# Grouped-query attention on one core: V loaded 8 KB per partition, scores in 32x64 tiles, PV by row halves, Q turned by a 0/1 matmul

## The chip, the core and the metric

The kernel runs on one core of a Trainium2 chip. The core has a matrix engine (TensorE, "PE" in the profile; its weight loads are listed apart as "PEld"), a vector engine (DVE), an activation engine (ACT), GpSimd (POOL) and a sync engine (SP) that issues all DMAs here. Sixteen DMA engines carry the data between HBM and the on-chip buffer SBUF. TensorE writes its results to PSUM, from where DVE or ACT have to fetch them. The metric is the device time of one execution in microseconds (us), as the median of several runs; lower is better.

## What is computed

```python
B, Hq, Hkv, Sq, Sk, D = 16, 32, 8, 16, 2048, 128      # q, k, v in bfloat16
def reference(q, k, v):
    rep = Hq // Hkv                                   # 4 query heads for one K/V head
    k = jnp.repeat(k, rep, axis=1)
    v = jnp.repeat(v, rep, axis=1)
    scores = jnp.einsum("bhqd,bhkd->bhqk", q, k) * D ** -0.5
    p = softmax(scores, axis=-1)
    return jnp.einsum("bhqk,bhkd->bhqd", p, v)
```

There are 128 K/V heads (16 x 8). Each has 64 query rows (4 query heads x 16 positions), 2048 keys of 128 numbers, and as many values. K and V are 67 MB each and every byte is used once, so the data has to stream through.

## The kernel before, in words

**Units.** A *quad* is four K/V heads, and there are NQD = 32 of them; a *pair p* is two heads, and there are NP = 64. K comes a quad at a time (2 MB, 16 KB in each of 128 partitions, a head in 32 partitions), V a pair at a time (1 MB). For V the 2048 keys of a head are spread over all 128 partitions, 16 keys in each, so a partition gets 4 KB for each of the two heads. Q comes in chunks of 16 heads (8 pairs).

**Stages of the work.**
- *KT* (line 351, DVE): 32x32 transposes turn half of a quad's keys into KT, as fp32 words that hold two bf16 numbers each. The head stays in its 32 partitions, and the 128 dimensions lie as 32 partitions x 2 (b) x 2 (e). Two instructions for each score step.
- *Q* (line 174; DVE for chunk 0, POOL for the rest): `lay_q` lays Q out with zeros at the other heads' places (Q4), through a mask. TensorE turns it (line 278: four stages of four fp32 transposes for a chunk) and ACT copies it out of PSUM into QT (line 404).
- *S(n)* (lines 300 and 256, TensorE): scores of half of a quad's keys for its four heads. A matmul has 64 contraction rows (two heads, with a block-diagonal Q of 128 columns) and 512 keys; two row tiles (64x128) run side by side. 16 matmuls; every second group uses weights that are already loaded (line 256).
- *Sneg* (line 373, DVE): two instructions fetch S(n) from PSUM, scale it by minus the softmax scale and keep the minimum; every second n a small instruction (line 381) makes the softmax shift of the quad.
- *exp(p)* (line 413, ACT): 2048 exponentials for each row, with the row sum.
- *PT* (line 312, TensorE): eight fp32 transposes turn the exponentials of a pair in two halves of four; ACT copies each half out of PSUM (line 423). The two halves and the Q stages share NSTAGE = 3 PSUM banks in turn (`free(u)` waits until the use three earlier has been copied out).
- *PV(p)*: 16 keys of each partition. In the wide form (line 330) one matmul has both heads' weights (128 columns) and both heads' values (256 columns), and half of its result is not used. In the narrow form (line 336) there are two column tiles of 64, one for each head. `both_heads` (line 29) takes the wide form in three pairs out of four until the last eight pairs.
- *norm(p)* (lines 436 and 440, ACT; the last five on DVE, line 394): result times the reciprocal of the row sum (line 359), then a 32 KB store.

**Order.** Each engine runs its list in order, and semaphores tie the lists. `pe_prog` and `act_prog` are written by one loop (lines 136 to 145): for p it emits S(p+2), exp(p), PV(p-4), norm(p-4), the two halves PT(p), and in the steps p = 2, 3, 4, 5 of eight one of the four Q stages. The first score step of a chunk, S(8c), waits for the last Q copy (line 287). DVE runs Sneg of n and then KT of n+2. PV(p) waits until norm(p-1) has emptied the one PSUM bank of results (line 322).

**DMA.** SP issues everything in one list (lines 238 to 247). K has NK = 3 buffers and waits for the KT of three quads earlier, V has NV = 7 buffers of one pair and waits for the PV of seven pairs earlier, stores wait for their norm. The last pair's V comes in two parts (LASTV).

## Time and profile before

| | |
|---|---|
| median of 3 runs | 342.75 us (342.29 to 343.37) |
| span of the profiled execution | 340.7 us, so some 2 us lie around it |
| PE busy | 304.3 us (89%) |
| DVE busy | 304.8 us (89%) |
| ACT busy | 253.6 us (74%) |
| DMA | 138.87 MB, mean 408 GB/s; 16 engines 99.5% covered by packets |
| granted TensorE clock | 0.5 between 12 and 24 us, 1.00 from 27 us on |

The main loop repeats every eight pairs, with the chunk of Q: the first score step of a chunk starts at 54.19, 94.02, 133.83, 173.65, 213.47, 253.29 and 293.11 us, so a period is 39.82 us and one pair 4.98 us. "Busy" for PE covers the way of a matmul through the array, so starts of successive groups say more than durations. In a row of the timeline the first number is the start, the second the time until the last of its instructions has ended, and the bracket holds the idle time of the engine just before and what ended it.

### The profile page before, as it was taken

The numbers are of one execution on the slowest core, as the hardware profiler recorded it, in microseconds if no ns is written. First come the engines' busy times: TensorE is split into PE (matmuls) and PEld (weight loads), VectorE is DVE, ScalarE is ACT, GpSimd is POOL, SyncE is SP. The second block draws the span as 40 slices with busy tenths as digits, with TensorE's granted clock in tenths as the row PEclk, the third lists the DMA queues.
The fourth block names the chain that finished last, engine by engine and source line by source line (L and its number), as shares of the span: only waits on it lengthen the run. The fifth ranks groups of instructions, "written<-read, shape, count | busy, mean of one in ns | idle before, by whom it ended". The sixth has DMA issues, their size and how long they took to land.

```text
span 340.7 us, 7084 instructions
## 1 busy us (share of the span) xinstructions
PE 304.3 (89%) x3040; PEld 182.4 (54%) x2528; DVE 304.8 (89%) x457; ACT 253.6 (74%) x390; POOL 81.3 (24%) x40
## 2 busy tenths in 40 slices
PE   3466798999899998999989999999989999899987
PEld 3012355555655664566555556556645665555556
DVE  1879998999989997999989999899979999899952
ACT  3025776789777888778867897778887788678875
POOL 2840007500092004900075000920039000000000
PEclk9759999999999999999999999999999999999999
DMA  7999999999999999999999999999999999999993
GB/s 294 443 415 420 425 415 414 411 419 422 424 423 410 415 419 424 416 420 407 419 426 423 419 405 417 421 428 415 412 418 416 426 418 423 408 419 415 410 407 121
DMA packets 32688, 138.87 MB, mean 408 GB/s; under 512 B 10896, under 2 KB 11152, under 8 KB 28560
## 3 DMA queue, kind: packets, MB, share of 16 engines
q1 hardware_dynamic: 32656, 138.42, 99.5%
q8 instruction: 22, 0.36, 0.4%
q14 instruction: 10, 0.08, 0.1%
HBM read 136.31 MB, written 2.10 MB: 406 GB/s over the span
## 4 chain that ended last, share of the span: by engine, by line
PE 55%; DVE 28%; ACT 9%; issue 5%; DMA 2%; ACTq 0%; SPq 0%; DVEq 0%
PE O_ps L330 17%; DVE Sneg L373 17%; PE S_ps L300 14%; PE S_ps L256 12%; DVE KT L351 11%; PE ST_ps L312 8%; ACT P L413 4%; ACT QT L404 2%; DMA Kn<-in_k_dram 2%; PE ST_ps L278 2%; ACT PT L423 2%; ACT O L436 1%; PE S_ps L336 1%; PE O_ps L336 1%; DVE rrec L359 0%
## 5 line engine op out<-in xcount | busy, mean ns | idle before, releaser
L373 DVE TENSOR_SCALAR_CACHE_REDUCE Sneg<-S_ps 128x1024 f32<-128x1024 f32 x128 | 150.7, 1213 | 19.1 <-PE S_ps L256 18.9
L351 DVE STREAM_TRANSPOSE KT<-Kn 128x1024 f32<-128x1024 f32 x128 | 150.8, 1217 | 3.9 <-DMA Kn<-in_k_dram 3.9
L413 ACT ACTIVATE P<-Sneg,nbias 128x2048 bf16<-128x2048 f32 x64 | 128.2, 2004 | 16.1 <-DVE nbias L381 15.1
L300 PE MATMUL S_ps<-KT,QT 64*128 64x512 bf16 x512 | 103.5, 394 | 24.1 <-DVE Sneg L373 12.8
L174 POOL TENSOR_SCALAR Q<-Qn,mask 128x1024 bf16<-128x1024 bf16 x28 | 79.1, 2843 | 181.1 <-PE ST_ps L278 174.6
L256 PE MATMUL S_ps<-KT,QT 64*128 64x512 bf16 x512 | 103.1, 392 | 0.0
L330 PEld LDWEIGHTS O_ps<-Vb,PT 128*128 128x128 bf16 x672 | 62.4, 98 | 34.7 <-issue 28.0
L330 PE MATMUL O_ps<-Vb,PT 128*128 128x256 bf16 x672 | 80.7, 273 | 0.0
L423 ACT ACTIVATE PT<-ST_ps 128x512 f32<-128x512 f32 x128 | 69.3, 595 | 13.1 <-PE ST_ps L312 12.1
L300 PEld LDWEIGHTS S_ps<-KT,QT 64*128 64x128 bf16 x512 | 27.4, 94 | 93.7 <-issue 72.4
L312 PE MATMUL ST_ps<-ident,P 128*128 128x128 f32 x512 | 67.6, 275 | 4.1 <-ACT P L413 4.1
L436 ACT ACTIVATE O<-O_ps,rrec 64x128 bf16<-64x128 f32 x84 | 30.4, 362 | 46.2 <-PE O_ps L330 45.7
L312 PEld LDWEIGHTS ST_ps<-ident,P 128*128 128x128 f32 x512 | 56.9, 141 | 10.3 <-ACT P L413 7.8
L278 PE MATMUL ST_ps<-ident,Q 128*128 128x128 f32 x128 | 20.4, 291 | 5.2 <-DVE Q L174 5.2
L404 ACT ACTIVATE QT<-ST_ps 128x512 f32<-128x512 f32 x32 | 19.3, 604 | 5.1 <-PE ST_ps L278 5.1
L336 PEld LDWEIGHTS O_ps<-Vb,PT 128*64 128x64 bf16 x576 | 16.7, 110 | 11.5 <-issue 11.5
L336 PE MATMUL O_ps<-Vb,PT 128*64 128x128 bf16 x576 | 19.5, 221 | 0.6 <-ACT O L440 0.6
L278 PEld LDWEIGHTS ST_ps<-ident,Q 128*128 128x128 f32 x128 | 16.4, 152 | 5.2 <-issue 5.2
L413 ACT ACTIVATION_READ_ACCUMULATOR P<-Sneg,nbias 128x1 f32 x64 | 12.2, 191 | 0.0
L373 DVE DVE_READ_ACCUMULATOR Sneg<-S_ps 128x1 f32 x128 | 10.6, 83 | 0.0
L440 ACT ACTIVATE O<-O_ps,rrec 128x128 bf16<-128x128 f32 x17 | 6.0, 351 | 2.2 <-PE O_ps L336 2.2
L381 DVE TENSOR_TENSOR nbias<-nhalf 128x2 f32<-128x2 f32 x32 | 5.1, 160 | 1.1
(19 smaller groups left out, 20.1 us busy)
## 6 DMA issues: line engine op xcount, KB each, us to landing
Kn<-in_k_dram SPq DMA_DIRECT2D x32, 2048.0 KB, 15.3
Vb<-in_v_dram SPq DMA_DIRECT2D x63, 1024.0 KB, 16.6
Qn<-in_q_dram SPq DMA_DIRECT2D x8, 256.0 KB, 13.3
out_dram<-O SPq DMA_DIRECT2D x64, 32.0 KB, 16.1
Vb<-in_v_dram SPq DMA_DIRECT2D x1, 768.0 KB, 12.0
Vb<-in_v_dram SPq DMA_DIRECT2D x1, 256.0 KB, 12.3
```

The source lines that it names most:

```text
L174: eng.tensor_scalar(Q4[:, :, :, r, :].rearrange("p j b x -> p (j b) x"), src, mask[:, r:r + 1], None, op0=ALU.mult,).then_inc(sem_q4, 1)
L256: return pe.add_instruction(mybir.InstMatmult(name=nc.get_next_instruction_name(), engine=mybir.EngineType.PE, ins=[pe.lower_ap(rhs), pe.l ...
L278: ins = pe.transpose(dst[:, 128 * j:128 * (j + 1)], src[:, 4 * x + j, b, :], ident4[:, :])
L300: ins = pe.matmul(s_ap, w, x, start=(acc == 0), stop=(acc == 3))
L312: ins = pe.transpose(dst[:, 128 * t:128 * (t + 1)], P[p % 2][:, 128 * x:128 * (x + 1)], ident4[:, :])
L330: ins = pe.matmul(O_ps[:, 0:256], pt[:, j // 2, j % 2, :], Vb[p % NV][:, :, j, :], start=(j == 0), stop=(j == J - 1),)
L336: ins = pe.matmul(o_ap(p)[64 * g:64 * (g + 1), :], pt[:, j // 2, j % 2, 64 * g:64 * (g + 1)], Vb[p % NV][:, g, j, :], start=(j == 0), stop ...
L351: dve.transpose(KT[n % NKT][:, :].rearrange("p (t b g e a) -> p e g t b a", t=J // 4, b=2, g=4, e=2)[:, e], Kn[Q % NK][:, :].bitcast(F32). ...
L373: dve.tensor_scalar(Sneg[p % NS][:, 1024 * x:1024 * (x + 1)].rearrange("p (t a m) -> p t a m", t=4, m=8), S_ps[:, 1024 * y:1024 * (y + 1)] ...
L413: act.activation(P[p % 2][:, :].bitcast(BF16), Sneg[p % NS][:, :], ACT.Exp, bias=nbias[:, p:p + 1], scale=-1.0, accum_out=rowsum[:, p:p + ...
L423: act.activation(PT[p % NPT][:, 4 * h:4 * (h + 1), :].rearrange("p t q -> p (t q)"), stage_ap(u), ACT.Copy,).then_inc(sem_ev, 1)
L436: ins = act.activation(Osb[p % NO][rows, :], O_ps[rows, 128 * g:128 * (g + 1)], ACT.Copy, scale=rrec[rows, p:p + 1])
```

## The change

- **V** comes with 8 KB of one head in each partition, a head in 64 partitions. The DMA is still 1 MB for two heads; its packets are 8 KB, where they were 4 KB. The buffers are NV = 4 of a quad (8 pairs' worth), each with two semaphores.
- **Scores** run in 32x64 tiles: a tile is one head, 32 contraction rows and 64 query columns. Four matmuls that follow each other have four different row groups; heads 0 and 2 write the two halves of the partitions of one PSUM bank, heads 1 and 3 those of another. 32 matmuls of 512 keys for each S, where there were 16.
- **exp** writes the two pairs of a quad side by side, so PT turns half h of the keys of all four heads; h takes the place of the pair in the lists, and PT(2n) needs both exp of quad n. In the loop PT runs one step later (`turn(p - 1)`).
- **PV by row halves**: PV(h) has 16 keys of each partition; for each key two matmuls with 64 contraction rows, one for each half of the partitions, each with 128 weight columns and 256 value columns, into two PSUM banks. From quad NEND = 28 on there are four 64x64 tiles for a key. `both_heads` is gone. PV runs five steps behind (PVLAG = 5) and waits for both V halves of the quad.
- **norm** runs once for a quad, as four ACT instructions of 64 partitions each.
- **Q** is turned by matmuls with a 0/1 matrix `fold` as moving operand (32 columns) and Q as weights: two stages of 16 matmuls for a chunk, at steps 3 and 5 of eight (QAT), and two ACT copies. POOL makes `fold` with two more instructions at the start.
- **PSUM**: two staging banks (NSTAGE = 2) where there were three, two result banks where there was one.
- **End**: the last copies are divided between ACT and DVE, the last two halves are staged in S_ps, the last V comes in three parts of a quad.

The diff, cut to its core:

```diff
-NV = 7
+NV = 4
-NSTAGE = 3
+NSTAGE = 2
-PVLAG = 4
-SLAG = 14
+PVLAG = 5
+SLAG = 8
+QAT = (3, 5)
-LASTV = ((0, 12), (12, 16))
-NFAST = 8
-NLATE = 5
-def both_heads(p, NP):
-    return p < NP - NFAST and p % 4 != 3
+LASTV = ((0, 16), (16, 28), (28, 32))
+NEND = 28
...
-    vf = v.rearrange("b h s d -> (b h) (s d)").rearrange("g (a x) -> a g x", a=128)
+    vf = v.rearrange("b h s d -> (b h s d)").rearrange("(n a x) -> n a x", n=NT, a=128)
...
-    for p in range(NP - 2):
+    for p in range(NT - 2):
         pe_prog.append(("S", p + 2))
         exp(p)
-        if p >= PVLAG:
-            pv(p - PVLAG)
-            norm(p - PVLAG)
-        act_prog += turn(p)
+        upto = p - PVLAG + (p >= NT - 4)
+        while due <= upto:
+            pv(due)
+            if due % 2 and due // 2 < NEND:
+                norm(due // 2)
+            due += 1
+        if p >= 1:
+            turn(p - 1)
         c, i = divmod(p, 8)
-        if c + 1 < NQC and 2 <= i < 6:
-            q_part(c + 1, i - 2)
+        if c + 1 < NQC and i in QAT:
+            q_part(c + 1, QAT.index(i))
...
+    turn(NT - 2, ("act", "dve"))
+    turn(NT - 1, ("act", "dve"))
+    pv(NT - 2)
+    pv(NT - 1)
+    act_prog.append(("norm", NQD - 1, (0,)))
+    dve_prog.append(("norm", NQD - 1, (1,)))
...
-                if p < NP - 1:
-                    dst = Vb[s][:, :, :, :].rearrange("a g j d -> a g (j d)")
-                    sp.dma_start(dst, vf[:, 2 * p:2 * p + 2, :]).then_inc(sem_v[s], 16)
+                if n >= NV and c == 0:
+                    sp.wait_ge(sem_pv, 2 * (n - NV) + 2)
+                if n < NQD - 1:
+                    dst = Vb[s][:, c, :, :].rearrange("a j d -> a (j d)")
+                    sp.dma_start(dst, vf[p]).then_inc(sem_v[s][c], 16)
...
                 if op[0] == "QT":
-                    for j in range(4):
-                        ins = pe.transpose(dst[:, 128 * j:128 * (j + 1)], src[:, 4 * x + j, b, :], ident4[:, :])
+                    for j in range(8):
+                        for e in range(2):
+                            z = 2 * j + e
+                            ins = pe.matmul(dst[:, 32 * z:32 * (z + 1)], src[:, j, b, e, :], mv, start=True, stop=True)
...
-                            for y in range(2):
-                                rows = slice(64 * y, 64 * (y + 1))
-                                s_ap = S_ps[:, 512 * (2 * y + u):512 * (2 * y + u + 1)]
-                                w = qt[rows, b, e, 128 * (i + y):128 * (i + y + 1)]
-                                x = kt[rows, b, e, 2 * u:2 * (u + 1), :]
+                            for g in (0, 2, 1, 3):
+                                rows = slice(32 * g, 32 * (g + 1))
+                                col, y = 64 * (g // 2), g % 2
+                                s_ap = S_ps[col:col + 64, 512 * (2 * y + u):512 * (2 * y + u + 1)]
+                                w = QT[c % 2][rows, b, i, :, e]
+                                x = kt[rows, b, e, 4 * u:4 * (u + 1), :]
...
-                        if both_heads(p, NP):
-                            ins = pe.matmul(
-                                O_ps[:, 0:256], pt[:, j // 2, j % 2, :], Vb[p % NV][:, :, j, :],
-                                start=(j == 0), stop=(j == J - 1),
-                            )
+                        if n < NEND:
+                            for x in range(2):
+                                rows = slice(64 * x, 64 * (x + 1))
+                                ins = pe.matmul(
+                                    o_ap(n, x)[:, 0:256], w[rows].rearrange("p c q -> p (c q)"), Vb[n % NV][rows, :, key, :],
+                                    start=(key == 0), stop=(key == 31),
+                                )
...
-                    if both_heads(p, NP):
-                        for g in range(2):
+                    for x in xs:
+                        for c in range(2):
```

## The prediction

> **What bounds the kernel now.** I read the waits first, then the busy times of one period of the main loop, then the starts in its timeline, and last the DMA.

> The waits (who waited for whom: us in total, times, longest):

> ```profile
> PE S_ps L300 <- DVE Sneg L373: 12.8, 15, 2.6
> PE S_ps L300 <- ACT QT L404: 8.5, 7, 1.2
> PE ST_ps L312 <- ACT P L413: 4.1, 15, 0.3
> DVE KT L351 <- DMA Kn<-in_k_dram: 3.9, 1, 3.9
> ```

> The last line matters most: no engine waits for data after the first load of K, and no line of PV waits for V. The loop is set by engines that wait for each other.

> Busy times by stretch (length, then PE, PEld, DVE, ACT, POOL, granted clock, DMA share, GB/s):

> ```profile
> 9.50:24.00 14.50, 7.50 (x38) 1.39 (x20) 12.23 (x16) 0.93 (x1) 11.31 (x4) 0.59 1.00 425
> 94.00:133.80 39.80, 37.80 (x368) 22.93 (x304) 37.65 (x57) 32.01 (x51) 11.29 (x5) 1.00 1.02 417
> 321.00:331.00 10.00, 9.05 (x144) 5.39 (x128) 7.29 (x14) 7.37 (x12) 0.00 (x0) 1.00 1.03 410
> ```

> The middle line is a period of eight pairs: PE 37.80 and DVE 37.65 of 39.80 us, ACT 32. PE and DVE are both nearly full, and the DMA engines are covered too (1.02), though nobody waits for them. So the DMA stream runs just beside the engines. What a PE step really takes comes from starts in the timeline:

> ```profile
> 101.91 1.09 PE L312 MATMUL ST_ps<-ident,P 128*128 128x128 f32 x8 [0.26 <-ACT P L413]
> 102.60 1.09 ACT L423 ACTIVATE PT<-ST_ps 128x512 f32<-128x512 f32 x2 [0.49 <-PE ST_ps L312]
> 103.20 0.40 PE L300 MATMUL S_ps<-KT,QT 64*128 64x512 bf16 x2 [0.19 <-DVE Sneg L373]
> 103.57 2.00 ACT L413 ACTIVATE P<-Sneg,nbias 128x2048 bf16<-128x2048 f32 x1
> 104.77 0.40 PE L256 MATMUL S_ps<-KT,QT 64*128 64x512 bf16 x2
> 105.11 1.92 PE L330 MATMUL O_ps<-Vb,PT 128*128 128x256 bf16 x16
> 106.86 1.04 PE L312 MATMUL ST_ps<-ident,P 128*128 128x128 f32 x8
> ...
> 111.61 1.04 PE L312 MATMUL ST_ps<-ident,P 128*128 128x128 f32 x8
> 112.58 0.40 PE L300 MATMUL S_ps<-KT,QT 64*128 64x512 bf16 x2
> ...
> 116.24 1.04 PE L312 MATMUL ST_ps<-ident,P 128*128 128x128 f32 x8
> 117.12 0.60 PE L278 MATMUL ST_ps<-ident,Q 128*128 128x128 f32 x4
> 117.65 0.40 PE L300 MATMUL S_ps<-KT,QT 64*128 64x512 bf16 x2
> ...
> 322.91 1.08 PE L336 MATMUL O_ps<-Vb,PT 128*64 128x128 bf16 x32
> 323.93 1.09 PE L312 MATMUL ST_ps<-ident,P 128*128 128x128 f32 x8
> ```

> From start to start: S to PV 105.11 - 103.20 = 1.91; wide PV to PT 106.86 - 105.11 = 1.75; narrow PV to PT 323.93 - 322.91 = 1.02; PT to S 112.58 - 111.61 = 0.97; a Q stage adds 117.65 - 116.24 - 0.97 = 0.44. A period is 8 x 1.91 + 6 x 1.75 + 2 x 1.02 + 8 x 0.97 + 4 x 0.44 = 37.34; the other 2.48 of 39.82 are PE's waits. The largest is 1.2 at each chunk's first S, for the Q copy on ACT.

> **The change, part by part.** Spacings first. A group of two score tiles (512 columns) comes every (104.77 - 103.20) / 7 = 0.224. The wide PV (one tile, 256 columns, 273 ns each by its group) comes every (1.92 - 0.273) / 15 = 0.110; narrow pairs (128 columns, 219 ns) every (1.08 - 0.219) / 15 = 0.057. Two tiles side by side thus cost what one does, plus 0.002 to 0.004.

> *Scores.* 32 matmuls for 16, four at a time for two: eight groups as before. No row shows four tiles. Low end: the wide PV's rate, 0.220, so S 1.88; high end: 0.010 for the two further tiles, so 1.99. I take 1.91, as the row nearest to it. No gain: the columns to stream are the same.

> *PV by row halves.* 32 matmuls of 256 columns, two at a time: 16 groups at 0.110 to 0.115, as long as the wide form, but now in all eight pairs of a period. The two narrow ones go: +2 x 0.73 = 1.46. A change of tile form also has a price: the last S group starts at 104.77, would be through at 104.99, and PV starts at 105.11, so 0.12; narrow PV to PT loses 0.10 (its last pair starts at 323.77). Wide PV to PT loses nothing. After the change PV and PT differ in form: 1.75 + 0.10 = 1.85 (1.75 to 1.95).

> *Q by matmul.* Two stages of 16 loads with 32 moving columns. Bounds: 0.029 each (narrow PV, 64 loads and matmuls as 32 x 0.029) and 0.109 (fp32 transposes, 0.88 for eight): a stage 0.46 to 1.75. Loads in bf16 stand nearer the first; I take 0.75, 1.50 in a period for 1.76.

> *Sum of PE steps:* 8 x (1.91 + 1.85 + 0.97) + 1.50 = 39.34 for 37.34.

> *Waits on PE.* (a) S of a new chunk is still right behind the last Q stage. PE could go on 0.85 after that stage's start; the copy ends at 0.95 + 0.61 + 0.12 = 1.68, so 0.8 (before 1.2). (b) Two staging banks: the Q stage takes the bank of PT's first half. ACT starts that copy 0.69 after PT's start (101.91, 102.60) and takes 0.55, so the bank is free at 1.36; PE is there at 0.88: 0.45, twice a period. (c) PT(2n) waits for the quad's second exp. On ACT, from the start of that quad's S: exp at 0.37 to 2.5, norm from PV's end at 3.9, now four instructions, 1.5; two copies 1.1, so 6.5; second exp to 8.6. PE is there after 4.73 + 1.91 + 1.85 = 8.5: 0.2 with the signal's way, four times. Behind PT in PE's list stand the next S and PV, so these waits pass through. Together 0.8 + 0.9 + 0.8 = 2.5 (1.7 to 3.5): as before.

> *Period:* 39.34 + 2.5 = 41.84, +2.0. The chain up to 42.8 us is DVE's at the slow clock and stays; from there to the end of the wide PVs (315 us) are 6.9 periods: 7 x 2.0 = +14.

> *DVE, ACT, SP.* KT and Sneg keep number and size; only their access order differs: 0. DVE alone would allow 37.65 a period. ACT has four 64-partition norm instructions for a quad as before, and two Q copies less (2 x 0.6), on an engine with 7 us to spare. Stores are two for a quad as before. SP's V load waits for a whole quad's PV, but V has 8 pairs of room for 7; stores behind it wait with it, and their output buffers hold the same eight pairs.

> *V packets.* K alone (9.5 to 24 us, 16 KB packets) moves 425 GB/s at share 1.00, V alone (321 to 331, 4 KB) 410 / 1.03 = 398. A 1 MB load: 2.64 against 2.47. A cost for each packet would give 8 KB two thirds of the 0.17: 0.11 x 64 = 7 us less of the DMA stream (0 to 11). It lies beside the engines, which never waited: 0 now. It would count only if the engines got faster.

> *Ends.* The last four copies (2.04 on ACT) are divided over two engines, -0.9; the first narrow PV waits for norm 27 in the loop's last steps, about +1. POOL's two extra instructions end before the first Q is laid out. 0 +- 2.

> *Sum:* the execution's 340.7 + 14 = 355; with 2 us around it (342.75 against 340.7) **357 us**. Each 0.08 on S or PV is 7 x 8 x 0.08 = 4.5 us; the forecast's own range is 347 to 368.

> **Rivals.**

> *Faster.* The place is PE's list: if four tiles stream at the wide PV's rate (1.88), the change of form costs nothing (1.75), a Q stage takes 0.46 and the waits are 1.7, the period is 8 x 4.60 + 0.92 + 1.7 = 39.3, -0.5 x 7, so 339. It decides from a period under 39.8. The stream lets it: the last part of V is issued at 324.45 and lands 12.3 later, at 336.8, the end comes 3.9 later; 7 less is 334 + 2 = 336. For it: PE's streams were never longer than their columns by more than 0.01. Against it: all four ends at once, and two narrow PVs gone for certain.

> *Dearer tiles.* S 2.05, PV 2.0, Q 1.0, waits 3.0: 8 x 5.02 + 2.0 + 3.0 = 45.2, +38: 380; half of it, 368. Against it stands the small price of the second tile.

> *Two tiles of one bank in turn.* Heads 0 and 2 write one bank from different row groups. If these took turns, each group would need two rounds: 8 x 0.224 = 1.79 a pair, 64 x 1.79 = 115: 472 us. Against it: narrow PV's two column tiles write one bank, at 0.057 a pair and not 0.110; but they share their rows. [...]

> *No change.* The faster and the dearer terms cancel: 343.

> **How the numbers follow.** Forecast 0.57, faster 0.20, dearer 0.12, in turn 0.05, no change 0.06. A difference under 0.3% (1 us) can't be told from none. Slower 0.57 + 0.12 + 0.05 = 0.74, faster 0.20, same 0.06. The range 340 to 371 leaves out half of the faster case and the upper half of dearer tiles and the turns, about 0.2.

> **What would show it.** Right: starts of successive first S 41 to 43 us apart; S to PV near 1.91; PV to PT near 1.85 in all pairs; PT and the Q stage waiting for ACT; DVE idle more than 2.2 us a period, for S; V's DMA share under 1.0. Wrong: a period under 39.8, KT or PV waiting for DMA, S to PV under 1.8 or over 2.1, or DVE or ACT rows that grew with their new access order.

## The result and the profile after

| | before | after |
| --- | --- | --- |
| median, us | 343.06 (342.29 to 345.75) | 361.88 (361.46 to 364.0) |
| ratio to before | | 1.056, 95% interval 1.051 to 1.061 |
| profiled execution: span, us | 340.7 | 360.4 |
| first S of pair 8 / of pair 56, us | 54.19 / 293.11 | 55.14 / 302.96 |
| period of eight pairs, us | 39.82 | 41.30 |
| start of S(62) / of S(63), us | 321.0 / 325.75 | 332.01 / 339.58 |
| instructions | 7,084 | 10,702 |

The changed kernel is 5.6% slower. The starts in the timeline divide the 19.7 us of span: 0.95 by pair 8, then six periods of +1.49, 8.9; 1.2 from S(56) to S(62); 2.8 from S(62) to S(63); 5.9 from there to the end. So about 11 us are the loop's and 8.7 the end's.

First the waits of the changed kernel (who waited for whom: us in total, times, longest):

```profile
PE S_ps L349 <- DVE Sneg L433: 12.5, 7, 2.6
...
PEld ST_ps L362 <- ACT P L482: 7.9, 27, 0.3
...
PE S_ps L349 <- ACT QT L472: 5.4, 7, 0.8
...
PE ST_ps L328 <- ACT PT L490: 4.2, 14, 0.3
...
DVE KT L411 <- DMA Kn<-in_k_dram: 3.9, 1, 3.9
...
PE O_ps L399 <- ACT O L500: 1.7, 1, 1.7
```

PE's seven waits for Sneg all lie before 49 us now (15 before, nine of them later), and the wait for the Q copy is 0.8 where it was 1.2. PT's wait for exp was there before, too (0.3, 15 times); it now comes at every second pair and shows at PE's weight loads. New are the wait of the Q stage for a staging bank (0.3 each) and one wait of PV for a norm near the end. Data are waited for once, at the start, as before.

Now one period (length, then PE, PEld, DVE, ACT, POOL, granted clock, DMA share, GB/s):

```profile
96.44:137.75 41.31, 39.90 (x609) 23.37 (x482) 38.18 (x57) 32.01 (x51) 11.31 (x5) 1.00 1.02 420
```

PE is busy 2.1 us longer than in the period of before (37.80), DVE 0.5 and ACT nothing. In the page's chain of the work that ended last PE has 83% of the span and DVE 7%, where it was 55% and 28%. PE's steps in the timeline, one pair and the next, then a Q stage and the first S of a chunk:

```profile
101.25 0.42 PE L349 MATMUL S_ps<-KT,QT 32*64 32x512 bf16 x4
101.50 0.39 PE L302 MATMUL S_ps<-KT,QT 32*64 32x512 bf16 x4
101.73 0.39 PE L349 MATMUL S_ps<-KT,QT 32*64 32x512 bf16 x4
...
103.18 1.92 PE L391 MATMUL O_ps<-Vb,PT 64*128 64x256 bf16 x32
105.11 1.09 PE L362 MATMUL ST_ps<-ident,P 128*128 128x128 f32 x8
106.13 0.42 PE L349 MATMUL S_ps<-KT,QT 32*64 32x512 bf16 x4
...
108.06 1.92 PE L391 MATMUL O_ps<-Vb,PT 64*128 64x256 bf16 x32
109.91 1.09 PE L362 MATMUL ST_ps<-ident,P 128*128 128x128 f32 x8
...
136.40 0.57 PE L328 MATMUL ST_ps<-fold,Q 128*128 128x32 bf16 x16 [0.25 <-ACT PT L490]
137.75 0.42 PE L349 MATMUL S_ps<-KT,QT 32*64 32x512 bf16 x4 [0.78 <-ACT QT L472]
```

Read from start to start: S to PV 1.93; PV to PT 1.85 (109.91 - 108.06), or 1.93 where PT waits for exp; PT to S 1.02; Q stage to S 1.35, of which 0.48 is the stage and 0.87 the wait for its copy. Four score tiles come every 0.225 us (101.73 - 101.50).

The end looks different. PE's rows after the last S:

```profile
337.54 1.09 PE L399 MATMUL O_ps<-Vb,PT 64*64 64x128 bf16 x64 [1.68 <-ACT O L500]
...
345.57 1.98 PE L399 MATMUL S_ps<-Vb,PT 64*64 64x128 bf16 x127 [0.20 <-issue]
349.02 1.81 PE L399 MATMUL S_ps<-Vb,PT 64*64 64x128 bf16 x114 [1.47 <-issue]
350.76 1.09 PE L362 MATMUL ST_ps<-ident,P 128*128 128x128 f32 x8
351.69 0.71 PE L362 MATMUL S_ps<-ident,P 128*128 128x128 f32 x5
352.73 0.55 PE L362 MATMUL S_ps<-ident,P 128*128 128x128 f32 x3 [0.33 <-issue]
353.20 1.93 PE L399 MATMUL O_ps<-Vb,PT 64*64 64x128 bf16 x123
356.62 0.27 PE L399 MATMUL O_ps<-Vb,PT 64*64 64x128 bf16 x5 [1.48 <-issue]
```

PE stops four times in the middle of its own list, for 3.48 us together, and the releaser is "issue": nothing that another engine did. The counts tell where: 127 matmuls between the first and the second stop, 114 + 8 + 5 = 127 to the third, 3 + 123 = 126 to the fourth. Each has a weight load of its own, so a stop comes every 252 to 254 instructions. The list of queues has the data's, q1, and one of instructions, q8 (packets, MB, share):

```profile
q1 hardware_dynamic: 24720, 138.42, 93.8%
q8 instruction: 36, 0.59, 0.6%
```

0.59 MB in 36 packets is 16 KB each. It moved 22 such packets before, 0.36 MB; PE's loads and matmuls grew with them, from 5,568 to 9,216, so there are 253 to 256 for each packet, about as many as between two stops. The data queue's share was 99.5% before and is 93.8% now, but the slack lies at the end: in the loop the engines' share is 1.02 as before, and it falls only behind 315 us, when the last K has landed. The data of a period are 17.3 MB (16.8 of K and V, 0.5 of Q and results); at the 420 GB/s of the row above they take 41.2 us, so the stream is still as long as the period. That the engines set the period shows in SP's list, which waits 69.0 us for V buffers (22.4 before), while no engine waits for data.

### The profile page after: what moved, and what is told of

Same layout as the page of the kernel before. It is cut to its first block, busy times and chain, and to the rows that moved or that the text cites. A ratio compares the mean times of both kernels' runs of the same rounds, so it can differ in the third digit from the quotient of the medians.

```text
span 360.4 us, 10702 instructions
## 1 busy us (share of the span) xinstructions
PE 318.5 (88%) x5120; PEld 184.5 (51%) x4096; DVE 311.4 (86%) x463; ACT 249.7 (69%) x382; POOL 82.1 (23%) x42
## 3 DMA queue, kind: packets, MB, share of 16 engines
q1 hardware_dynamic: 24720, 138.42, 93.8%
## 4 chain that ended last, share of the span: by engine, by line
PE 83%; DVE 7%; ACT 4%; issue 2%; DMA 2%; SPq 0%
PE O_ps L391 29%; PE S_ps L349 18%; PE S_ps L302 16%; PE ST_ps L362 16%; DVE Sneg L433 5%; DVE KT L411 3%; ACT PT L490 2%; DMA Kn<-in_k_dram 2%; PE ST_ps L328 2%; PE O_ps L399 1%; ACT QT L472 1%; PE S_ps L399 1%; ACT O L500 0%; PE S_ps L362 0%; SPq L269 0%
## 5 line engine op out<-in xcount | busy, mean ns | idle before, releaser
L433 DVE TENSOR_SCALAR_CACHE_REDUCE Sneg<-S_ps 128x1024 f32<-128x1024 f32 x128 | 151.5, 1221 | 29.2 <-PE S_ps L302 26.5
L411 DVE STREAM_TRANSPOSE KT<-Kn 128x1024 f32<-128x1024 f32 x128 | 150.8, 1217 | 3.9 <-DMA Kn<-in_k_dram 3.9
L349 PE MATMUL S_ps<-KT,QT 32*64 32x512 bf16 x1024 | 105.9, 398 | 23.1 <-DVE Sneg L433 12.5
L391 PE MATMUL O_ps<-Vb,PT 64*128 64x256 bf16 x1792 | 107.6, 270 | 0.0
L391 PEld LDWEIGHTS O_ps<-Vb,PT 64*128 64x128 bf16 x1792 | 82.8, 94 | 45.9 <-issue 19.0
L302 PE MATMUL S_ps<-KT,QT 32*64 32x512 bf16 x1024 | 104.8, 393 | 0.0
L490 ACT ACTIVATE PT<-ST_ps 128x512 f32<-128x512 f32 x123 | 67.0, 595 | 38.3 <-PE ST_ps L362 37.6
L349 PEld LDWEIGHTS S_ps<-KT,QT 32*64 32x64 bf16 x1024 | 31.0, 105 | 88.9 <-issue 68.9
L500 ACT ACTIVATE O<-O_ps,rrec 64x128 bf16<-64x128 f32 (+1 forms) x113 | 41.0, 363 | 44.0 <-PE O_ps L391 38.9
L328 PE MATMUL ST_ps<-fold,Q 128*128 128x32 bf16 x256 | 8.8, 178 | 9.5 <-DVE Q L207 5.3
L472 ACT ACTIVATE QT<-ST_ps 128x512 bf16<-128x512 f32 x16 | 9.4, 597 | 6.8 <-PE ST_ps L328 6.8
L328 PEld LDWEIGHTS ST_ps<-fold,Q 128*128 128x128 bf16 x256 | 7.6, 98 | 12.6 <-issue 9.1
L399 PE MATMUL O_ps<-Vb,PT 64*64 64x128 bf16 x256 | 4.4, 217 | 3.2 <-ACT O L500 1.7
L399 PE MATMUL S_ps<-Vb,PT 64*64 64x128 bf16 x256 | 4.2, 217 | 1.7 <-issue 1.7
```

Source lines behind the costliest of these rows:

```text
L302: return pe.add_instruction(mybir.InstMatmult(name=nc.get_next_instruction_name(), engine=mybir.EngineType.PE, ins=[pe.lower_ap(rhs), pe.l ...
L328: ins = pe.matmul(dst[:, 32 * z:32 * (z + 1)], src[:, j, b, e, :], mv, start=True, stop=True)
L349: ins = pe.matmul(s_ap, w, x, start=(acc == 0), stop=(acc == 3))
L391: ins = pe.matmul(o_ap(n, x)[:, 0:256], w[rows].rearrange("p c q -> p (c q)"), Vb[n % NV][rows, :, key, :], start=(key == 0), stop=(key == ...
L399: ins = pe.matmul(o_ap(n, x)[64 * c:64 * (c + 1), 0:128], w[rows, c], Vb[n % NV][rows, c, key, :], start=(key == 0), stop=(key == 31),)
L411: dve.transpose(KT[n % NKT][:, :].rearrange("p (t b g e a) -> p e g t b a", t=8, b=2, g=2, e=2)[:, e], Kn[Q % NK][:, :].bitcast(F32).rearr ...
```

## The experiments

Each run alters one part, of the changed kernel (e1 to e4, e6, e8, e9) or of the kernel before (e5, e7, e10). Ratios are to the kernel before.

### e1: narrow PV for every fourth quad

```diff
-                        if n < NEND:
+                        if n < NEND and n % 4 != 3:
```

The condition is replaced in PV and in the norm, which for such a quad becomes two 128-partition instructions.

> The changed kernel with the narrow PV (four 64x64 tiles for each key) in every fourth quad, that is in two pairs of eight, as often as before the change; its norm is then two ACT instructions for four. Theory (PE's list sets the loop, and the wide PV in all pairs is what lengthened it): each narrow half goes from 1.86 to 1.02 us, 2 x 0.84 = 1.7 less in a period of 41.3, of which waits for exp give back up to half: a period of 39.6 to 40.5, 352 to 357 us. Rival (the loop is set by the order ACT-PE, not by PE's sum): the period stays within 0.3 of 41.3, 360 to 362 us.

Measured: 360.12 us (358.6 to 361.22), ratio 1.051 (1.048 to 1.055); period 41.05. The theory missed, the rival held. PE's rows beside the two narrow pairs show where the saving went:

```profile
123.62 1.09 PE L403 MATMUL O_ps<-Vb,PT 64*64 64x128 bf16 x64
125.56 1.09 PE L366 MATMUL ST_ps<-ident,P 128*128 128x128 f32 x8 [0.84 <-ACT P L486]
...
132.03 0.42 PE L353 MATMUL S_ps<-KT,QT 32*64 32x512 bf16 x4 [0.53 <-DVE Sneg L437]
```

The first PV ends 0.8 us earlier, and PT then waits 0.84 for exp; the second saving turns into 0.53 of waiting for Sneg. A shorter PE step in one place isn't a shorter period: PE meets ACT and DVE at the next signal.

### e2: narrow PV everywhere

```diff
-                        if n < NEND:
+                        if False:
```

> The changed kernel with the narrow PV in all quads. Theory: 8 x 0.84 = 6.7 less on PE in a period, so PE has about 33 us of work and DVE (37.6) and the V and K stream take over: a period of 38 to 39.5, 338 to 345 us; DVE KT then waits for K now and then. Rival A (four times as many PV instructions, 128 for a half where the wide form has 64, cannot be fetched in time in the loop either): pauses of 1.5 us inside PV as at the end of the run, a period over 41, 360 us or more. Rival B (a less busy PE gets a lower clock): granted clock under 0.95, over 360 us.

Measured: 369.76 us (368.63 to 371.4), ratio 1.081 (1.077 to 1.084), granted clock 0.941; 14,230 instructions. The theory missed. (A narrow half has 128 loads and matmuls for 64 of a wide one, so twice as many, not the four times of rival A.) Where PE runs undisturbed a pair mostly takes 4.6 to 4.9 us, about 38 a period; but 14 times its list stops for more than 0.7 us, counted from start to start and ended by "issue", 26.4 us in all. One such place:

```profile
150.97 1.03 PE L403 MATMUL O_ps<-Vb,PT 64*64 64x128 bf16 x59
154.77 0.30 PE L403 MATMUL O_ps<-Vb,PT 64*64 64x128 bf16 x5 [2.77 <-issue]
155.00 1.76 PE L366 MATMUL ST_ps<-ident,P 128*128 128x128 f32 x8
156.69 0.64 PE L353 MATMUL S_ps<-KT,QT 32*64 32x512 bf16 x4
157.13 0.63 PE L306 MATMUL S_ps<-KT,QT 32*64 32x512 bf16 x4
```

Two losses are seen in turn. PE stops for 2.77 us inside a PV, released by "issue"; after that the score groups come every 0.44 us (157.13 - 156.69) in place of 0.225, and the granted clock is 0.91 on average from 150 to 170 us. Fetch and clock, offered as rivals, are both seen here, the second behind the first.

### e3: V in 4 KB packets again

```diff
-                    dst = Vb[s][:, c, :, :].rearrange("a j d -> a (j d)")
-                    sp.dma_start(dst, vf[p]).then_inc(sem_v[s][c], 16)
+                    for z in range(2):
+                        dst = Vb[s][:, c, 16 * z:16 * (z + 1), :].rearrange("a j d -> a (j d)")
+                        sp.dma_start(dst, vf[p][:, 2048 * z:2048 * (z + 1)]).then_inc(sem_v[s][c], 16)
```

> The changed kernel with V in packets of 4 KB again: each 1 MB load as two DMAs of 16 keys per partition. Theory (the stream lies beside the engines): no difference, 361 to 363 us, period 41.3, and the DMA's share rises a little. Rival (the larger packets are worth something already): 2 to 6 us longer, with KT or PV waiting for loads.

Measured: 361.81 us (359.87 to 363.08), ratio 1.057 (1.053 to 1.060), period 41.29. The theory held. This is the time of the changed kernel: in it, the larger packets of V are worth nothing. They do save something, in a place that nobody waits for; the stream's queue is busy 95.2% of 359.8 us for 93.8% of 360.4, 342.5 against 338.1, so 4.4 us.

### e4: wide PV to the last quad but one

```diff
-                        if n < NEND:
+                        if n != 31:
```

DVE's norm of quads 28 to 30 becomes four half-row instructions.

> The changed kernel with the wide PV in quads 28 to 30 as well (norm on DVE as four half-row instructions for a quad); only the last quad is narrow. Theory (the 1.5 us pauses inside the narrow PVs at the end are PE waiting for its next block of instructions: 128 loads and matmuls for a half in 1.0 us): the pause at 347 goes, since a wide half has 64 instructions in 1.8 us; the six wide halves cost 0.84 more each, so the total is between 2 us less and 3 us more. Rival (the pauses come from four 64x64 tiles or the banks they write): the pause in the last quad stays and the one in front of it goes as well, so this run alone tells only through the last quad: with the fetch theory that quad's pause moves or shrinks too, since fewer instructions were used up ahead of it.

Measured: 364.38 us (364.24 to 364.4), ratio 1.064 (1.063 to 1.066). The stops behind the last S are gone; the only gap over 0.7 us inside PV is the 1.67 us before PV(56), which waits for the norm of quad 27. The theory held: the time is paid back by the wide form itself, six halves at 1.77 to 1.86 us for 1.02. Of the 2.0 us between the two profiled spans, 0.9 lies ahead of pair 8, where the two kernels do the same, and 1.1 at the end. So the narrow form at the end costs less than the wide one even with its stops, by about 1 us.

### e5: the kernel before with the wide PV in all pairs

```diff
-    return p < NP - NFAST and p % 4 != 3
+    return p < NP - NFAST
```

> The kernel before with one part of the change alone: the wide PV in all pairs up to the last eight, so that the two narrow pairs of a period (1.02 us from PV to PT) become wide (1.75). Theory, the working of the prediction: PE's steps grow by 2 x 0.73 = 1.46 us a period, PE is the engine that sets the period, and at least two thirds of it come through: period 40.8 to 41.3 us for 39.82, time 349 to 354 us, so that this part alone is most of what the loop lost. Rival: the waits (a third of them for DVE's Sneg) take it up, as they took up the saving of two narrow pairs in e1: period 39.8 to 40.3, time 342.5 to 346 us, and the loop's loss comes from the new tile forms and banks.

Measured: 345.18 us (343.6 to 346.25), ratio 1.006 (1.003 to 1.009); period 40.13. The rival held. The stretch of one period, columns as above:

```profile
93.45:133.58 40.13, 38.92 (x336) 24.10 (x273) 37.84 (x57) 33.22 (x53) 11.31 (x5) 1.00 1.02 418
```

PE's steps grew by 1.46 as worked out (eight times 1.76 from PV to PT), but the period by 0.31: PE's waits for exp and Sneg fell by the rest. Of the 1.49 us that the change adds to a period, the loss of the two narrow pairs is 0.31 by itself, in the order and with the banks of the kernel before.

### e6: the Q stages one step earlier

```diff
-QAT = (3, 5)
+QAT = (2, 4)
...
-                    if t == max(0, 8 * c - QLEAD):
+                    if t == max(0, 8 * c - QLEAD - 2 * (c > 1)):
```

> The changed kernel with both Q stages one step earlier in PE's list (after pairs 2 and 4 of a chunk instead of 3 and 5), so that a whole pair lies between the last Q copy and the first S that needs it; the load of Q is issued two steps earlier with it. Theory: the wait of that S for the Q copy, 0.8 us a chunk, leaves the path: period 40.5 us for 41.30, time 355.5 to 357.5 us. Rival: the exp and the Sneg that the next steps wait for come no earlier, and the 0.8 turns up again as a longer wait of PT or S: period 41.1 to 41.4, time 360 to 362.5 us.

Measured: 365.19 us (364.61 to 365.8), ratio 1.064 (1.061 to 1.067); period 42.16. It missed both ways: slower, not faster or equal. The wait of the Q stage in the list of waits, its row in PE's timeline, and ACT's rows beside it:

```profile
PE ST_ps L328 <- ACT PT L490: 15.3, 14, 1.3
```

```profile
121.80 0.55 PE L328 MATMUL ST_ps<-fold,Q 128*128 128x32 bf16 x16 [1.27 <-ACT PT L490]
```

```profile
119.54 1.49 ACT L500 ACTIVATE O<-O_ps,rrec 64x128 bf16<-64x128 f32 x4 [1.15 <-PE O_ps L391]
121.06 1.09 ACT L490 ACTIVATE PT<-ST_ps 128x512 f32<-128x512 f32 x2
122.39 0.60 ACT L472 ACTIVATE QT<-ST_ps 128x512 bf16<-128x512 f32 x1 [0.24 <-PE ST_ps L328]
```

S no longer waits for the Q copy. But after an even pair ACT has four norm instructions (1.49 us) ahead of the PT copies, and the Q stage needs the bank that the first of those copies empties. With two staging banks it waits 1.1 us on average (1.3 at most) instead of 0.3, twice a period.

### e7: the kernel before with its Q stages one step earlier

```diff
-        if c + 1 < NQC and 2 <= i < 6:
-            q_part(c + 1, i - 2)
+        if c + 1 < NQC and 1 <= i < 5:
+            q_part(c + 1, i - 1)
```

> The kernel before with its four Q stages one step earlier each. There S waits 8.5 us in all for the Q copy, seven times. Theory: these 1.2 us a chunk leave the path, and the period falls from 39.82 towards the 37.65 that DVE is busy, by 0.6 to 1.2 us: time 336 to 340 us. Rival: the DMA stream, covered 99.5 per cent of the loop, holds the period as soon as the engines stop doing so: the last part of V lands when it did, KT or PV begin to wait for a load, time 341.5 to 343.5 us.

Measured: 342.13 us (341.94 to 344.37), ratio 0.998 (0.996 to 1.000). The rival held, and two stretches of the run show both sides of it:

```profile
90.20:128.84 38.64, 37.76 (x371) 22.96 (x306) 37.74 (x57) 32.05 (x51) 11.32 (x5) 1.00 1.02 418
247.43:290.03 42.60, 38.02 (x368) 23.21 (x305) 37.71 (x57) 32.93 (x52) 9.93 (x4) 1.00 1.03 420
```

```profile
DVE KT L351 <- DMA Kn<-in_k_dram: 14.2, 13, 3.6
```

Early on a period takes 38.64 us, 1.18 less than before, which is the wait that was taken away (1.2). The engines have then run ahead of the loads: later periods take up to 42.60 with the same busy times, and KT waits 14.2 us for K. The data queue is busy for 99.7% of the span. The time is that of the kernel before; with the stream busy for 339.3 of 340.3 us, the engines' gain can't show.

### e8: e2 with little V

```diff
+                if NV <= n < NQD - 1:
+                    return
                 if n < NQD - 1:
```

The V loads of quads 4 to 30 are left out, and those quads multiply by the V that is there.

Measured: 346.28 us (345.22 to 346.51 three times and 351.93 once), ratio 1.008 (1.005 to 1.011), granted clock 0.973; a period 38.8 us for e2's 43.4 (mean of the last five, from S to S). Stops over 0.7 us, counted as in e2: six, 8.4 us in all, for fourteen and 26.4. The stretch of the loop, in e8 and then in e2:

```profile
95.00:250.00 155.00, 134.26 (x3458) 79.10 (x2944) 150.53 (x225) 112.88 (x169) 45.25 (x16) 1.00 0.65 233
```

```profile
95.00:250.00 155.00, 126.80 (x3024) 71.85 (x2573) 130.96 (x196) 98.81 (x148) 45.21 (x16) 0.93 1.00 401
```

With the DMA share at 0.65 the clock stays at 1.00 and PE issues 14% more matmuls in the same time. So in the loop the stops come from the stream beside the instruction queue, as the first theory had it, though the sum stayed above its 5 us and the time above its 342. At the end of e8 the stops stand as they did:

```profile
333.31 1.81 PE L405 MATMUL S_ps<-Vb,PT 64*64 64x128 bf16 x114 [1.29 <-issue]
...
340.90 0.27 PE L405 MATMUL O_ps<-Vb,PT 64*64 64x128 bf16 x5 [1.48 <-issue]
```

These are the same two places as in the changed kernel's end (x114, x5), where the DMA share is 0.20 from 344 to 358 us. So those stops come with little data beside the instruction queue: in the changed kernel its packets land 3.5 to 4.0 us apart there, and PE runs through 252 to 254 instructions in some 2 us, the first rival's reading.

### e9: the Q stages two steps earlier

```diff
-QAT = (3, 5)
+QAT = (1, 3)
```

Chunk 0 keeps (3, 5); the load of Q is issued two steps earlier, as in e6.

> The changed kernel with its Q stages after pairs 1 and 3 of a chunk (3 and 5 in the changed kernel, 2 and 4 in e6; chunk 0 keeps 3 and 5). After odd pairs ACT has no norm ahead of the PT copy, which held up the Q stages of e6 (1.3 us each). Theory: the Q stages wait for the PT copy as in the changed kernel (0.3 each) and S no longer waits for the Q copy: period 40.3 to 40.7 us for 41.30, time 355 to 358 us; what e6 lost is then the place in ACT's list and not the earlier Q. Rival: a stage anywhere but where it stood costs as much as it saves, since only two staging banks stand between PE and ACT: period 41.1 us or more, time 360 us or more.

Measured: 356.7 us (356.3 to 358.05), ratio 1.041 (1.038 to 1.045); period 40.44. The theory held. Its waits:

```profile
PE ST_ps L329 <- ACT PT L491: 4.2, 14, 0.3
...
PE S_ps L350 <- ACT QT L473: 0.8, 1, 0.8
```

The Q stage waits for the bank as in the changed kernel, and S waits for the Q copy once instead of seven times. That wait of 0.87 us a period was worth 5.2 us, and e6's loss was the place in ACT's list.

### e10: e7 with V in 2 KB packets

```diff
+                    for z in range(2):
+                        dst = Vb[s][:, :, 8 * z:8 * (z + 1), :].rearrange("a g j d -> a g (j d)")
+                        src = vf[:, 2 * p:2 * p + 2, 1024 * z:1024 * (z + 1)]
+                        sp.dma_start(dst, src).then_inc(sem_v[s], 16)
```

> The kernel of e7 (before, Q stages one step earlier) with each V load as two DMAs whose packets have 2 KB where 4 KB stood. In the trace a 4 KB packet takes 161 ns and one of 8 KB 312, so a packet costs some 10 ns beyond its bytes; 16,384 more packets over 16 engines are 10 us of the stream. Theory: in e7 the stream sets the end, so this price, which was hidden in the changed kernel (e3), comes through in full: 349 to 354 us for 342.1, with KT waiting for K. Rival: the stream of e7 has slack in spite of its 99.7 per cent, or the packets cost nothing: 341.5 to 344 us.

Measured: 350.29 us (349.8 to 350.88), ratio 1.022 (1.019 to 1.026); KT waits 20.1 us for K. The theory held. Smaller packets cost 8 us here, of the 10 worked out, and nothing in e3: the same kind of cost, with and without a cover.

## Why the prediction was right, and where it was not

*Direction and size.* Forecast 357, measured 361.88, in the range and on the expected side. Two errors of opposite sign stand behind that, so how near it came is partly luck: with the ends as forecast the loop alone gives 354, and with the loop as forecast these ends give 366.

*PE's steps: right as a sum, not in its terms.* Forecast 39.34 us a period. Measured 8 x (1.93 + 1.85 + 1.025) + 2 x 0.48 = 39.4. PV to PT came out at the 1.85 that was put together from the wide rate and 0.10 for the change of tile form: inside a PV the pairs of matmuls still come every (1.92 - 0.270) / 15 = 0.110, so 16 of them fill 1.76, and the other 0.09 lie at the change. e5 gives the counterpart, 1.76 without such a change. No run takes this price away by itself, so that it belongs to the change of form is read from starts alone. S is 0.02 dearer than taken. The Q stage was mis-sized: 0.48 for 0.75, at the low end of its bounds, where the narrow PV's load and matmul (0.029 a pair) had put it. PT to S was taken as unchanged at 0.97 and is 1.02, 0.4 us a period that the sum left out; that the change of form is paid on that side as well is an estimate from these starts. The two cancel.

*Waits: each in its place, (c) too large.* (a) S for the Q copy 0.87 for a forecast 0.8, and e9 confirms it as path time by taking it away. (b) The bank 0.42 and 0.32 for 0.45 each; e6 shows how steep this price is when ACT is a little later. (c) PT for exp was put at 0.2 a time. The wait shown is 0.3, but PT starts only 0.08 later than where there is none (1.93 against 1.85). By these starts it lies mostly beside the 0.10 that the change of form takes at the same point, and the two delays don't add. Together 1.93 for 2.5, so the period is 41.30 and not 41.84: steps +2.06 and waits -0.55 against the period of before. The term "7 x 2.0 = +14" measured about +11.

*"Two narrow ones go: +2 x 0.73 = 1.46".* Right for PE's steps, and e5 shows that by itself it is worth 0.31, because waits shrink with it. The prediction's sum of steps plus waits holds only with the waits worked out anew for the changed kernel, as (a) to (c) did. The chain of steps alone would have been wrong in e1 and e5.

*V packets: right, the saving mis-sized.* Hidden, 0 us, and 4.4 us of the stream where 7 was put (e3). That it "would count only if the engines got faster" is what e7 and e10 show.

*DVE, ACT, SP: right.* Sneg 1,221 ns each for 1,213, KT 1,217 as before.

*Ends: the step that failed.* "0 +- 2" measured +8.7, in four parts. First, PV and PT run one step further behind S than before, and the end has to catch up: a wide PV(55) more between S(62) and S(63), 1.9 us, and a fourth PT behind S(63) where there were three, 1.0. The prediction had no term for this. Second, PV(56) waits 1.68 us for the norm of quad 27, while 0.73 of waiting for Sneg went from the same place; the prediction put this at about +1, against 0.9 won on the last copies. Third, behind S(63) 3.48 us are PE's stops at its own instructions, which no row of the kernel before that was read for the prediction had shown: there the narrow pairs stand in 32 matmuls, after it in 64 for the same columns. Fourth, 1.1 more lie between the last matmul and the end (2.4 to 3.5 us). The four make 8.5 of the 8.7.

*The rivals.* "Faster" had asked for four low ends at once: only the Q stage came there. (Its sum, 8 x 4.60 + 0.92 + 1.7, is 39.4 and not 39.3.) "Dearer tiles" needed S at 2.05 and fell with 1.93; its "half of it, 368" lies half way from 357 to 380, while half of the +38 would be 362. "No change" fell with the ratio. "Two tiles of one bank in turn" fell at once: four tiles on two banks come every 0.225 us, as two tiles did every 0.224.

*The signs.* The period, S to PV, PV to PT, the waits for ACT and DVE's idle time (41.31 - 38.18 = 3.1 us a period) came as listed. V's DMA share under 1.0 can't be read: no stretch of the changed kernel moves V alone at full rate, and the loop's share is 1.02 as before.

## What to carry to other kernels

Where an engine's period is steps plus waits, work out both anew: a step that is shortened or lengthened by 0.7 us moved the period by 0.1 to 0.2 here, while a wait in the right place came through in full (e7 early in its run, e9). Before larger packets or fewer instructions are weighed, see which of stream and engines is waited for: the same kind of packet cost was 0 us under the engines and 8 us under the stream. And count the instructions of a form, not only its columns: with twice the small matmuls for the same columns (e2) PE stopped in its own list for 26.4 us, and for 8.4 with the DMA share at 0.65 in place of 1.00 (e8).

## What the hardware showed that was not expected

At the end of the changed kernel PE stops every 252 to 254 instructions, a block in what follows, and a block takes it some 2 us (127 matmuls with their loads in 1.98). The stops end 3.45, 3.71 and 3.89 us apart (345.57, 349.02, 352.73, 356.62), with little data on the DMA (35% share from 340 to 358 us, most of it before 347). With the stream at full share (1.00 from 95 to 250 us), stops of 0.7 to 3.8 us appear in e2, where a block lasts about 6.4 us (1,779 loads and matmuls from 55 to 100 us); in the loop of the changed kernel a block lasts longer (about 1,090 loads and matmuls in 41.3 us, so 9.6) and none over 0.7 us were seen there.

The trace's records of single packets tie the stops at the end of the changed kernel to the fetch. The last four packets of the instruction queue land at 344.1, 347.6, 351.4 and 355.3 us, and PE goes on 1.3 to 1.5 us after each. The last three start 1.1 to 1.3 us after PE has entered the block before; with 0.9 to 1.3 us for the packet this makes the 3.5 to 3.9 us between stops.

After a stop of 2.77 us in e2 PE ran at about half its rate for a while (score groups 0.44 us apart for 0.225), after that of 1.47 us in the changed kernel it did not: the 114 matmuls behind it took 1.81 us, where 64 take 1.09, and the granted clock was 1.00 from 344 to 358 us. In e2 the clock was 0.91 on average from 150 to 170 us, and 0.93 from 95 to 250 us where e8, with fewer stops, had 1.00. So the stop at 152 us in e2 is paid twice.
